# Linear attention and an MLP mixer on one core: channel mixing's weight conversion bound to the key sums of head pairs 2, 3 and 4

## The chip, the core and the metric

The kernel runs on one core of a Trainium2 chip. TensorE (PE) multiplies matrices, VectorE (DVE), ScalarE (ACT) and GpSimd (POOL) do the elementwise work, and the queue of SyncE (SP) issues most DMAs. The metric is the time of one execution on the device in microseconds (us); lower is better.

## The reference

The first half is linear attention over 8 batches and 8 heads, 576 positions and 64 features a head. `phi` maps queries and keys to 256 positive features: a product with `w_phi` (64 x 128), less its largest absolute value along the features, then the exponentials of it and of its negative.

```python
q_p, k_p = (phi(q), phi(k))
kv = np.einsum('bhsf,bhsd->bhfd', k_p, v)
z = np.sum(k_p, axis=2)
num = np.einsum('bhsf,bhfd->bhsd', q_p, kv)
den = np.einsum('bhsf,bhf->bhs', q_p, z)[..., None] + 1e-06
```

The second half takes `num / den` as x (8 x 576 x 512) through two small networks. Token mixing: u = x + (relu(x^T w_tok1) w_tok2)^T with 256 hidden units. Channel mixing: out = u + relu(u w_ch1) w_ch2 with 1536 hidden units. The four weights of the mixers come as float64.

## The kernel before, in words

Work goes by head pairs: pair i holds two heads, and four pairs make a batch, so there are 32. For a pair, `less_max` (line 184) projects keys or queries and subtracts the largest absolute value, `keys` (line 246) takes exponentials, and `add_kv` (line 276) adds the products of key features and values to the PSUM tile pkv. When a pair is through, `nc.scalar.copy` on line 298 copies the sums to the tile kv, of which there is one for each part, so the sums of the next pair are copied only when the numerators of this one have read it. `turn` (line 336) transposes the queries and takes exponentials, `numerators` (line 363) multiplies them with kv, and the denominators' reciprocals are multiplied in on line 402. For the first 4 pairs (PLAIN) this is done in plain float32; later operands are split into a high and a low part for float32r. For the first 8 pairs (EARLY) each denominator goes out to memory and back by five or six small DMAs around the reciprocal (lines 391 to 400).

`token_mix` (line 416) handles a batch in two halves, each when its two pairs are attended; `channel_mix` (line 462) handles 256 positions at a time, in six blocks of up-projection (line 478, 48 matmuls each) and of down-projection (line 493), and needs batch 0 to be mixed for its first two turns. A block reads the weights converted so far: its `until` on line 504 asks for two more chunks of `wc2`.

`convert` (line 107) turns a float64 piece of up to 128 x 512 into a high and a low float32 part. It loads it to one of four staging tiles (tags late0 to late3) by SP's queue, and then runs one absolute value on ACT (line 124), four operations of bit arithmetic on DVE (lines 125 to 128), a cast on ACT (line 65) and a subtraction on POOL (line 68). The tile that it works on is called bitsc in the profile for channel mixing's weights, the staging tile rawc. `load_weights` (line 137) calls it 7 times for token mixing's weights and then 24 times for channel mixing's, in three groups of eight (line 153): four pieces of `wc1`, four of `wc2`.

The order is set in two steps. `weave` (line 547) runs five generators side by side, keys, queries, token mixing, weight loading and channel mixing, and goes on with the one whose own clock, advanced by the cost it yields over its share, is furthest behind; a generator that yields None waits. That gives the order in which instructions are traced. From it a list scheduler with a simulated timeline places each instruction on its engine's queue: an earlier traced one goes first, and a later one may fill a slot in which its operands are ready and its engine is free in the simulation. On the chip each engine's queue runs in exactly that order.

The weight loader yields 8.0 a piece (`pace`, line 134) until pair 3 is attended, then 1.0.

Of the kernel before, what the change touches and what calls it, by code (L numbers as in the profile page):

```python
# [8 lines left out]
F32 = mybir.dt.float32  # L9
# [3 lines left out]
AF = mybir.ActivationFunctionType  # L13
# [4 lines left out]
P = 128  # L18
# [7 lines left out]
PLAIN = 4  # L26
EARLY = 8
BORROWED = 18
STAGES = 4
LAST = 15  # L30
LAG = 0.02
# [11 lines left out]
def mixer_kernel(ctx, tc, qk, vm, vt, w_phi, w1, w2, wc1, wc2d, out):  # L43
    nc = tc.nc
# [17 lines left out]
    def split(hi, lo, raw, eng_hi, eng_lo):  # L62

        if eng_hi is nc.scalar:
            nc.scalar.copy(hi, raw)
        else:
            eng_hi.tensor_copy(hi, raw)
        eng_lo.tensor_tensor(lo, raw, hi.bitcast(F32), op=ALU.subtract)
# [28 lines left out]
    for j in range(2):  # L97
        t = odd.tile([P, 5, 2, D + 1], F32, tag=f"v{j}", name=f"v{j}", bufs=1)
# [4 lines left out]
        vtiles.append(t)  # L103

    nstage = [0]

    def convert(hi, lo, srcs, name, tag=None):

        w, n = hi.shape
        if tag is None:  # L110
            tag = f"late{nstage[0] % STAGES}"
            nstage[0] += 1
        raw = wk.tile([P, 4, 256], U32, tag=tag, name=f"raw{name}", bufs=3 if tag == "xt1" else 1)
        raw = raw.rearrange("p a b -> p (a b)")[:w, :2 * n]
        at = 0
        for src in srcs:
            m = src.shape[1]
            nc.sync.dma_start(raw[:, 2 * at:2 * (at + m)].bitcast(I64), src)
            at += m
        raw = raw.rearrange("p (n two) -> p n two", two=2)  # L120
        top, low = raw[:, :, 1], raw[:, :, 0]
        m = wk.tile([P, 512], U32, tag="bits", name=f"bits{name}", bufs=3)[:w, :n]

        nc.scalar.activation(m.bitcast(F32), top.bitcast(F32), AF.Abs)
        nc.vector.tensor_scalar(m.bitcast(F32), m.bitcast(F32), LEAST, MOST, op0=ALU.max, op1=ALU.min)
        nc.vector.tensor_scalar(m, m, 3, 0x3FFFFFF8, op0=ALU.logical_shift_left, op1=ALU.bitwise_and)
        nc.vector.scalar_tensor_tensor(m, top, 0xC0000000, m, op0=ALU.bitwise_and, op1=ALU.bitwise_or)
        nc.vector.scalar_tensor_tensor(m, low, 29, m, op0=ALU.logical_shift_right, op1=ALU.bitwise_or)
        split(hi, lo, m.bitcast(F32), nc.scalar, nc.gpsimd)

    def flat(t):
        return t.rearrange("p a b -> p (a b)")

    def pace():
        return 1.0 if NP - 1 in attended else 8.0

    def load_weights():
        for u in (0, 3):
            s = UNITS[u][2]
            convert(flat(w1_h[:, u:u + 2]), flat(w1_l[:, u:u + 2]),  # L140
                    [w1[s + o:s + o + P] for o in (0, P)], f"1_{u}")
            yield 1.0
        convert(w1_h[:D, 2], w1_l[:D, 2], [w1[512:]], "1_2")
        for w in (w1_h, w1_l):
            nc.scalar.copy(w[D:, 2], w[:D, 2].bitcast(F32))
        yield 0.4
        for u in range(NT):
            rows = w2[u * P:(u + 1) * P]
            convert(w2_h[:, u, :256], w2_l[:, u, :256], [rows[:, :256]], f"2_{u}")
            yield 0.5  # L150
            convert(w2_h[:, u, 256:], w2_l[:, u, 256:], [rows[:, 512:], rows[:, 256:512]], f"3_{u}")
            yield 0.7
        for e in range(0, E, 512):
            for c in range(NC_):
                convert(wc1_h[:, c, e:e + 512], wc1_l[:, c, e:e + 512],
                        [wc1[c * P:(c + 1) * P, e:e + 512]], f"c1_{c}_{e}")
                yield pace()
            for k in range(e // P, e // P + 4):
                src = wc2d[k * P:(k + 1) * P]
                late = k - (NE - STAGES)  # L160
                if late < 0:
                    t, tag = cst.tile([P, 2, C], F32R, name=f"wc2_{k}"), None
                else:
                    t = wk.tile([P, 2, C], F32R, tag=f"late{late}", name=f"wc2_{k}", bufs=1)
                    tag = f"late{late + 1}" if late + 1 < STAGES else "xt1"
                wc2.append(t)
                convert(t[:, 0], t[:, 1], [src], f"c2_{k}", tag)
                loaded.add(k)
                yield pace()

# [13 lines left out]
    def less_max(ts, units, name, base=None):  # L184
# [4 lines left out]
        if base == D:  # L189
            ps = ps_a.tile([P, 2, 2, F], F32, tag=f"a{nplain['k'] % 2}", name=f"pp{name}")  # L190
            nplain["k"] += 1
        elif base == 0 and (nplain["q"] % 2 == 0 or nplain["q"] >= BORROWED):
            ps = ps_h.tile([P, 2, 2, F], F32, tag="h", name=f"pp{name}")
# [52 lines left out]
    def keys():  # L246
        groups = [[(0, 0), (0, 1)], [(0, 2), (0, 3)], [(1, 0), (1, 1)], [(1, 2), (1, 3)], [None]]
        todo = None
        for i in range(B * NP):
            yield from until(lambda: i < 2 or i - 2 in asked)  # L250
            if i < PLAIN:
                load_plain(i)
            else:
                load(i)
            v_sb, queue = vtiles[i % 2], nc.sync if i else nc.scalar
            queue.dma_start(v_sb[:, 0:4].rearrange("p u j d -> p (u j) d")[:, :, :D], vm[i])
            for j in range(2):
                queue.dma_start(v_sb[j * D:(j + 1) * D, 4, j, :D], vt[i, j])
            plain = D if i < PLAIN else None
            ts = pairs[i] if i < PLAIN else stack(raws[i], D, f"k{i}")  # L260
            for g, us in enumerate(groups):
                pm = less_max(ts, us, f"k{i}_{g}", plain)
                kp = wk.tile([P, 2, 2, F], F32, tag="kp", name=f"kp{i}_{g}")
                for sg in range(2):
                    nc.scalar.activation(kp[:, :len(us), sg], pm[:, :len(us)], AF.Exp, scale=1.0 - 2.0 * sg)  # L265
                yield 0.22
                if todo:
                    add_kv(*todo)
                    yield 0.82
                todo = (i, g, us, kp, v_sb)  # L270
        add_kv(*todo)
        yield 0.82
# [3 lines left out]
    def add_kv(i, g, us, kp, v_sb):  # L276
        if g == 0:
            pkvs[0] = ps_k.tile([P, 2, 2, D + 1], F32, tag="kv", name=f"pkv{i}")
        pkv = pkvs[0]
        for n, u in enumerate(us):  # L280
            for sg in range(2):
                if u is None:
                    o = pkv[:, sg].rearrange("p j d -> p (j d)")
                    v = v_sb[:, 4].rearrange("p j d -> p (j d)")
                else:
                    o, v = pkv[:, sg, u[0]], v_sb[:, u[1], u[0]]
                nc.tensor.matmul(o, kp[:, n, sg], v, start=g == 0 and n == 0 and sg == 0, stop=u is None,  # L287
                                 skip_group_check=True)
        if g < 4:
            return  # L290

        both = []
        for k in range(1 if i < PLAIN else 2):
            kv = wk.tile([P, 2, 4, D], F32 if i < PLAIN else F32R, tag=f"kv{k}", name=f"kv{k}_{i}", bufs=1)
            for at, src in ((slice(0, 4, 3), pkv[:, :, :, :D]),
                            (slice(1, 3), pkv[:, :, :, D:].to_broadcast([P, 2, 2, D]))):
                if k == 0:
                    nc.scalar.copy(kv[:, :, at], src)
                else:
                    nc.vector.tensor_tensor(kv[:, :, at], src, both[0][:, :, at].bitcast(F32), op=ALU.subtract)  # L300
            both.append(kv)
        kvs[i] = both
# [103 lines left out]
    def until(cond):  # L406
        while not cond():
            yield None
# [138 lines left out]
    def weave(streams):  # L547
# [3 lines left out]
        while streams:  # L551
# [13 lines left out]

    weave([(keys(), 5.2, True), (queries(), 5.2, True), (token_stream(), 8.0, False),
           (load_weights(), 10.0, False), (channel_stream(), 19.5, False)])


# [40 lines left out]
```

## Time and profile before

| what | value |
|---|---|
| median of 3 runs | 1162.64 us (1160.67 to 1170.23) |
| the profiled execution's own time | 1164.33 us |
| its span, first to last instruction | 1162.2 us |
| TensorE busy | 1121.3 us, 96% |
| VectorE, ScalarE, GpSimd busy | 685.7, 659.4, 570.1 us |
| matmuls | 9032 |

The profile is of one execution. PE is the matmuls, PEld the weight loads that overlap them. Names such as pkv<-v,kp are tiles, written and read, with buffer numbers left out; L298 is a line of the kernel. A float32 matmul of the plain pairs is recorded as two matmuls. Matmuls are pipelined and their ends are modelled, so a shown duration can reach beyond the start of the next; the distance between starts is the pace.

### The profile page before, as it was taken

To read this page: it belongs to the slowest core of one execution; us is meant where nothing else is said; L and a number is where in the kernel's file an instruction comes from. 1 tells how busy PE (TensorE), PEld (TensorE's weight loads), DVE (VectorE), ACT (ScalarE), POOL (GpSimd) and SP (SyncE) were. 2 spreads that over 40 slices of the span, in tenths; PEclk is the share of its full clock that TensorE was granted. 3 is DMA by queue.
4 is the path that set the end of the run, shared out by engine and by line. 5 is a ranking of instruction groups with operands and counts; after the bars stand their busy time and mean duration, and the time that the engine had idled before them with its cause. 6 is when DMAs were issued, how large, how long until landed. Compare 5 with 4: busy or idle time off the path is not lost.

```text
span 1162.2 us, 24135 instructions
## 1 busy us (share of the span) xinstructions
PE 1121.3 (96%) x9032; PEld 1090.5 (94%) x9032; DVE 685.7 (59%) x1446; ACT 659.4 (57%) x1845; POOL 570.1 (49%) x734
## 2 busy tenths in 40 slices
PE   8987799999999999999999999999999999999998
PEld 7766699998999899999999999999999989999998
DVE  7989763536656665667566465573666666553111
ACT  5678785666656665666657465563655666441110
POOL 3347773555545564566646354563554655430000
PEclk9988999999999999999999999999999999999999
DMA  8564130111111011111111011110111110000000
GB/s 224 162 187 135 42 88 24 47 43 54 32 28 52 21 41 41 32 49 32 32 49 33 19 32 50 32 50 13 38 48 33 50 31 11 20 1 19 19 19 19
DMA packets 72531, 56.77 MB, mean 49 GB/s; under 512 B 49920, under 2 KB 63648, under 8 KB 72416
## 3 DMA queue, kind: packets, MB, share of 16 engines
q1 hardware_dynamic: 71056, 54.89, 16.7%
q8 instruction: 71, 1.16, 0.4%
q10 hardware_dynamic: 1360, 0.36, 0.2%
q14 instruction: 44, 0.36, 0.1%
HBM read 45.72 MB, written 9.51 MB: 48 GB/s over the span
## 4 chain that ended last, share of the span: by engine, by line
PE 85%; ACT 5%; DVE 4%; DMA 3%; issue 1%; POOL 1%; SPq 0%; POOLq 0%; DVEq 0%; ACTq 0%
PE acc L74 25%; PE h L74 25%; PE pkv L287 9%; PE pn L74 7%; PE ph L74 4%; PE pa L74 3%; PE pt L343 3%; PE ppk L205 2%; PE ppq L205 2%; DMA inv<-few 1%; PE px L423 1%; PE pn L377 1%; PE ppk L209 1%; ACT qh L356 1%; ACT qf L350 1%
## 5 line engine op out<-in xcount | busy, mean ns | idle before, releaser
L74 PE MATMUL acc<-gh,wc 128*128 128x256 f32 x1728 | 336.5, 282 | 0.2 <-ACT gh L489 0.2
L74 PEld LDWEIGHTS acc<-gh,wc 128*128 128x128 f32 x1728 | 274.0, 189 | 0.5 <-ACT gh L489 0.4
L74 PE MATMUL h<-ul,wc_h 128*128 128x256 f32 x864 | 243.4, 282 | 1.9 <-POOL ul L470 1.8
L74 PE MATMUL h<-uh,wc_h 128*128 128x256 f32 x864 | 244.8, 284 | 0.5 <-DVE gl L490 0.5
L74 PE MATMUL h<-uh,wc_l 128*128 128x256 f32 x864 | 243.7, 282 | 0.0
L74 PE MATMUL acc<-gl,wc 128*128 128x256 f32 x864 | 242.3, 282 | 0.0
L287 PE MATMUL pkv<-v,kp 128*128 128x65 f32 (+1 forms) x1152 | 165.7, 280 | 0.4 <-ACT kp L265 0.3
L74 PEld LDWEIGHTS h<-ul,wc_h 128*128 128x128 f32 x864 | 163.1, 189 | 2.7 <-POOL ul L470 2.7
L74 PEld LDWEIGHTS h<-uh,wc_h 128*128 128x128 f32 x864 | 162.6, 188 | 1.2 <-DVE gl L490 1.1
L74 PEld LDWEIGHTS h<-uh,wc_l 128*128 128x128 f32 x864 | 163.4, 189 | 0.0
L74 PEld LDWEIGHTS acc<-gl,wc 128*128 128x128 f32 x864 | 162.8, 188 | 0.0
L287 PEld LDWEIGHTS pkv<-v,kp 128*128 128x128 f32 x1152 | 156.9, 203 | 4.0 <-issue 1.8
L265 ACT ACTIVATE kp<-pmk 128x256 f32<-128x256 f32 (+1 forms) x320 | 109.3, 392 | 89.0 <-POOL pmk L221 83.7
L357 POOL TENSOR_TENSOR ql<-qf,qh 128x320 fp32r<-128x320 f32 (+1 forms) x112 | 92.8, 828 | 135.9 <-ACT qh L356 133.2
L490 DVE SCALAR_TENSOR_TENSOR gl<-h,gh 128x512 fp32r<-128x512 f32 x108 | 74.0, 686 | 140.3 <-ACT gh L489 139.6
L350 ACT ACTIVATE qf<-pt 128x320 f32<-128x320 f32 (+1 forms) x256 | 105.2, 414 | 84.6 <-PE pt L343 83.9
L489 ACT ACTIVATE gh<-h 128x512 fp32r<-128x512 f32 x108 | 64.6, 598 | 102.5 <-PE h L74 101.8
L74 PE MATMUL pn<-qh,kv 128*128 128x320 f32 (+1 forms) x448 | 114.9, 297 | 1.7 <-DVE pq L214 0.8
L402 POOL TENSOR_TENSOR xt<-xt,den 128x320 f32<-128x320 f32 x64 | 53.8, 840 | 116.7 <-DVE den L401 36.6
L357 DVE TENSOR_TENSOR ql<-qf,qh 128x320 fp32r<-128x320 f32 (+1 forms) x112 | 71.1, 635 | 65.0 <-ACT qh L356 64.6
L221 POOL TENSOR_TENSOR pmk<-pk,mxk 128x256 f32<-128x256 f32 (+1 forms) x140 | 86.8, 620 | 30.0 <-DVE mxk L219 23.2
L180 POOL TENSOR_TENSOR stq<-raw,stq 64x512 fp32r<-64x512 f32 (+1 forms) x56 | 79.8, 1424 | 40.5 <-ACT stq L179 36.4
(109 smaller groups left out, 2420.8 us busy)
## 6 DMA issues: line engine op xcount, KB each, us to landing
raw<-in_qk SPq DMA_DIRECT2D x27, 576.0 KB, 4.0
rawc<-in_wc SPq DMA_DIRECT2D x24, 512.0 KB, 4.8
v<-in_vm SPq DMA_DIRECT2D x31, 256.0 KB, 3.9
out_x<-xt SPq DMA_DIRECT2D x12, 256.0 KB, 2.2
out_x<-xt SPq DMA_DIRECT2D x16, 192.0 KB, 2.0
raw<-in_w SPq DMA_DIRECT2D x8, 256.0 KB, 3.5
out_x<-xt SPq DMA_DIRECT2D x16, 128.0 KB, 3.0
pair<-in_qk SPq DMA_DIRECT2D x8, 160.0 KB, 3.8
```

The costliest lines, as they stand in the source:

```text
L74: nc.tensor.matmul(o, a, m, start=first and i == 0, stop=last and i == 2, skip_group_check=group_ok)
L180: nc.gpsimd.tensor_tensor(t[lo:lo + D], src, t[base:base + D].bitcast(F32), op=ALU.subtract)
L205: nc.tensor.matmul(ps[:, i].rearrange("p two f -> p (two f)"), t[:, c:c + P], wp2.rearrange("p two f -> p (two f)"), start=True, stop=True)
L221: eng.tensor_tensor(pm[:, :n], pr, mx[:, :n].unsqueeze(2).to_broadcast([P, n, F]), op=ALU.subtract)
L265: nc.scalar.activation(kp[:, :len(us), sg], pm[:, :len(us)], AF.Exp, scale=1.0 - 2.0 * sg)
L287: nc.tensor.matmul(o, kp[:, n, sg], v, start=g == 0 and n == 0 and sg == 0, stop=u is None, skip_group_check=True)
L343: nc.tensor.transpose(ptr[:, n], r, ident)
L350: nc.scalar.activation(full, src, AF.Exp, scale=1.0 - 2.0 * sg)
L357: (nc.gpsimd if sg else nc.vector).tensor_tensor(lo, full, hi.bitcast(F32), op=ALU.subtract)
L402: nc.gpsimd.tensor_tensor(x, x, den, op=ALU.mult)
L489: nc.scalar.activation(gh, ph, AF.Relu)
L490: nc.vector.scalar_tensor_tensor(gl, ph, 0.0, gh.bitcast(F32), op0=ALU.max, op1=ALU.subtract)
```

## The change

The copy of a pair's key sums is kept under the pair's number in `summed`. The loader does not trace a group of eight conversions of channel mixing's weights before pair 2's (then 3's, 4's) sums have been traced, and each conversion's first instruction, the absolute value on ACT, gets an edge that places it behind that pair's copy in ACT's queue. The edge orders one engine's own instructions and carries no semaphore. Loads and token mixing's weights are as before.

```diff
--- before.py
+++ after.py
@@ -26,6 +26,7 @@
 PLAIN = 4
 EARLY = 8
 BORROWED = 18
+FROM = 2
 STAGES = 4
 LAST = 15
 LAG = 0.02
@@ -103,8 +104,9 @@
         vtiles.append(t)
 
     nstage = [0]
-
-    def convert(hi, lo, srcs, name, tag=None):
+    summed = {}
+
+    def convert(hi, lo, srcs, name, tag=None, behind=None):
 
         w, n = hi.shape
         if tag is None:
@@ -121,7 +123,8 @@
         top, low = raw[:, :, 1], raw[:, :, 0]
         m = wk.tile([P, 512], U32, tag="bits", name=f"bits{name}", bufs=3)[:w, :n]
 
-        nc.scalar.activation(m.bitcast(F32), top.bitcast(F32), AF.Abs)
+        with tc.issue_after(summed[behind].ins) if behind is not None else nullcontext():
+            nc.scalar.activation(m.bitcast(F32), top.bitcast(F32), AF.Abs)
         nc.vector.tensor_scalar(m.bitcast(F32), m.bitcast(F32), LEAST, MOST, op0=ALU.max, op1=ALU.min)
         nc.vector.tensor_scalar(m, m, 3, 0x3FFFFFF8, op0=ALU.logical_shift_left, op1=ALU.bitwise_and)
         nc.vector.scalar_tensor_tensor(m, top, 0xC0000000, m, op0=ALU.bitwise_and, op1=ALU.bitwise_or)
@@ -151,9 +154,11 @@
             convert(w2_h[:, u, 256:], w2_l[:, u, 256:], [rows[:, 512:], rows[:, 256:512]], f"3_{u}")
             yield 0.7
         for e in range(0, E, 512):
+            pair = FROM + e // 512
+            yield from until(lambda: pair in summed)
             for c in range(NC_):
                 convert(wc1_h[:, c, e:e + 512], wc1_l[:, c, e:e + 512],
-                        [wc1[c * P:(c + 1) * P, e:e + 512]], f"c1_{c}_{e}")
+                        [wc1[c * P:(c + 1) * P, e:e + 512]], f"c1_{c}_{e}", None, pair)
                 yield pace()
             for k in range(e // P, e // P + 4):
                 src = wc2d[k * P:(k + 1) * P]
@@ -164,7 +169,7 @@
                     t = wk.tile([P, 2, C], F32R, tag=f"late{late}", name=f"wc2_{k}", bufs=1)
                     tag = f"late{late + 1}" if late + 1 < STAGES else "xt1"
                 wc2.append(t)
-                convert(t[:, 0], t[:, 1], [src], f"c2_{k}", tag)
+                convert(t[:, 0], t[:, 1], [src], f"c2_{k}", tag, pair)
                 loaded.add(k)
                 yield pace()
 
@@ -295,7 +300,7 @@
             for at, src in ((slice(0, 4, 3), pkv[:, :, :, :D]),
                             (slice(1, 3), pkv[:, :, :, D:].to_broadcast([P, 2, 2, D]))):
                 if k == 0:
-                    nc.scalar.copy(kv[:, :, at], src)
+                    summed[i] = nc.scalar.copy(kv[:, :, at], src)
                 else:
                     nc.vector.tensor_tensor(kv[:, :, at], src, both[0][:, :, at].bitcast(F32), op=ALU.subtract)
             both.append(kv)
```

## Rows read from the trace of the kernel before

**Rows 1.** The page: its head line, the busy line of the engines, and PE's row of the 40 slices of 29.06 us each (a digit is the busy share in tenths).

```profile
span 1162.2 us, 24135 instructions
PE 1121.3 (96%) x9032; PEld 1090.5 (94%) x9032; DVE 685.7 (59%) x1446; ACT 659.4 (57%) x1845; POOL 570.1 (49%) x734
...
PE   8987799999999999999999999999999999999998
```

**Rows 2.** The windows of the first 200 us, all instructions. Columns: stretch, its length, then busy us and (number) of PE, PEld (weight load), DVE, ACT, POOL, then the granted clock, the DMA share and GB/s.

```profile
27.00:57.00 30.00, 29.70 (x104) 23.47 (x103) 29.18 (x58) 20.03 (x47) 11.43 (x8) 1.00 0.60 177
57.00:75.00 18.00, 14.58 (x95) 11.65 (x93) 15.29 (x34) 16.07 (x40) 9.57 (x7) 1.00 0.57 172
75.00:100.00 25.00, 19.24 (x91) 15.50 (x91) 23.02 (x42) 16.61 (x40) 11.87 (x10) 0.80 0.68 177
100.00:125.00 25.00, 21.02 (x126) 17.82 (x126) 24.02 (x46) 20.59 (x52) 18.35 (x16) 0.90 0.37 109
125.00:145.00 20.00, 15.90 (x109) 13.81 (x109) 11.98 (x30) 16.04 (x46) 16.70 (x20) 0.96 0.08 18
145.00:165.00 20.00, 19.94 (x167) 19.73 (x167) 13.88 (x35) 15.98 (x45) 13.71 (x18) 1.00 0.30 87
165.00:200.00 35.00, 34.94 (x301) 34.74 (x301) 13.26 (x31) 22.02 (x65) 18.60 (x28) 1.00 0.13 36
```

**Rows 3.** The windows of the same stretches, only instructions that read or write the conversion's tile bitsc. Columns: stretch, its length, busy us and (number) of DVE, ACT, POOL, then clock, DMA share, GB/s of the stretch.

```profile
27.00:57.00 30.00, 22.73 (x32) 9.46 (x15) 9.42 (x6) 1.00 0.60 177
57.00:75.00 18.00, 9.34 (x13) 5.00 (x8) 5.68 (x4) 1.00 0.57 172
75.00:100.00 25.00, 19.51 (x26) 8.27 (x13) 8.99 (x7) 0.80 0.68 177
100.00:125.00 25.00, 17.95 (x21) 5.59 (x9) 6.76 (x5) 0.90 0.37 109
125.00:145.00 20.00, 0.00 (x0) 0.62 (x1) 2.57 (x2) 0.96 0.08 18
145.00:165.00 20.00, 2.21 (x4) 1.34 (x2) 1.28 (x1) 1.00 0.30 87
```

**Rows 4.** The chain of waits from 20 to 160 us, pieces in order of time: start, us, what ran.

```profile
37.74 3.60 PE pkv L287 x16
...
54.25 2.50 PE pn L377 x4
...
63.17 1.73 PE pkv L287 x16
```

**Rows 5.** Who waited for whom between 60 and 125 us: us in total, times, the longest.

```profile
PE ppq L209 <- DVE pmq L221: 5.4, 2, 3.7
...
PE ppt L209 <- DVE pmq L221: 3.4, 1, 3.4
```

**Rows 6.** The timeline of PE in the first 180 us: start, us, engine and line, operation, tiles, shapes, count, and in brackets the idle time before it and what ended it.

```profile
68.28 0.61 PE L287 MATMUL pkv<-v,kp 128*128 128x130 f32 x4
...
74.76 0.48 PE L209 MATMUL ppt<-wp,pair 64*128 64x128 f32 x2 [3.42 <-DVE pmq L221]
...
115.97 1.08 PE L377 MATMUL pn<-qf,kv 128*128 128x256 f32 x4
```

**Rows 7.** The timeline of DVE in the wait at 71 us, same columns; the instruction after these two is pmq.

```profile
71.62 1.08 DVE L127 SCALAR_TENSOR_TENSOR bitsc<-rawc,bitsc 128x512 uint32<-128x512 uint32 x1
72.62 1.75 DVE L126 TENSOR_SCALAR bitsc<-bitsc 128x512 uint32<-128x512 uint32 x1
```

**Rows 8.** The windows of 5 us behind that wait, all instructions, columns as in the second group.

```profile
75.00:80.00 5.00, 5.00 (x22) 4.38 (x22) 5.00 (x12) 2.60 (x7) 2.03 (x2) 0.54 0.79 193
80.00:85.00 5.00, 5.00 (x27) 3.98 (x26) 4.97 (x8) 2.71 (x6) 2.26 (x2) 0.78 0.99 225
```

**Rows 9.** The timeline of PE where channel mixing begins in earnest (the first of the 20 up-projection matmuls that run between 149.7 and 155 us).

```profile
149.74 0.28 PE L74 MATMUL h<-uh,wc_h 128*128 128x256 f32 x1
```

**Rows 10.** The timeline of POOL: one low-part subtraction of the key split beside the wait at 71 us, and the last product of batch 0 with its reciprocals.

```profile
72.23 1.86 POOL L180 TENSOR_TENSOR stk<-raw,stk 64x640 fp32r<-64x640 f32 x1
...
132.93 0.73 POOL L402 TENSOR_TENSOR xt<-xt,den 128x256 f32<-128x256 f32 x1 [0.86 <-DMA den<-inv]
```

**Rows 11.** The conversion's first instruction, one of its four on DVE and its last, over the whole span, by the tile bitsc: duration ns min/median/max, first and last start in us, shapes.

```profile
L124 ACT ACTIVATE bitsc<-rawc x24: 657/672/709, 27.1 to 154.4; 128x512 f32<-128x512 f32 x24
L126 DVE TENSOR_SCALAR bitsc<-bitsc x24: 408/424/1751, 28.9 to 156.3; 128x512 uint32<-128x512 uint32 x24
L68 POOL TENSOR_TENSOR wc_l<-bitsc,wc_h x12: 1269/1506/1799, 33.6 to 114.2; 128x512 fp32r<-128x512 f32 x12
```

**Rows 12.** The timeline of ACT: the copies of the key sums of pairs 2 and 3, and of pair 4 (two instructions each).

```profile
72.97 0.65 ACT L298 COPY kv<-pkv 128x256 f32<-128x256 f32 x2
...
100.62 0.64 ACT L298 COPY kv<-pkv 128x256 f32<-128x256 f32 x2
...
127.49 0.64 ACT L298 CAST kv<-pkv 128x256 fp32r<-128x256 f32 x2
```

**Rows 13.** The loads of channel mixing's weights, from the view by the tile rawc.

```profile
DMA to landing us min/median/max: 3.7/4.8/5.6
```

**Rows 14.** The window of channel mixing's first blocks, PE's instructions on the tile h alone (48 matmuls per block of up-projection). Columns: stretch, length, busy us and (number) of PE, clock, DMA share, GB/s.

```profile
120.00:214.00 94.00, 26.03 (x184) 0.98 0.18 50
```

## The prediction

> **What bounds the kernel now.** I read the busy line and the slices first [rows 1]: TensorE is busy for 96% of the span and its digit is 9 from the eighth slice (203 us) on. So a change to weight work that is over by 165 us can pay or cost only ahead of that, and I cut the start into stretches by what happens there [rows 2], with the conversions' own share of them [rows 3]. The reader is to see four things.
>
> From 27 to 57 us PE and DVE are both full: PE 29.70 of 30 us, DVE 29.18, of which 22.73 is conversion. The chain of waits says which of them sets the pace: it runs along PE, matmul to matmul [rows 4]. PE is slow there: 16 of the key-sum matmuls take 3.60 us at 37.74 and 1.73 us at 63.17. The clock column prints 1.00 for this stretch, but that spacing is the lower of the two levels (1.2 against 2.4 GHz); the rise comes at about 57 us, behind a run of numerators and transposes.
>
> From 57 to 145 us PE is no longer full: it idles 3.42, 5.76, 3.98 and 4.10 us in the four stretches, 17.3 us in all [rows 2]. The largest waits are for DVE's less-max, 5.4 and 3.4 us [rows 5]. One is seen whole at 70.9 to 74.8 us [rows 6]: PE waits for pmq, and pmq stands in DVE's queue behind two conversion instructions of 1.08 and 1.75 us [rows 7]. The clock then falls: 0.54 granted in the next 5 us, 0.78 in the 5 after [rows 8].
>
> From 125 to 145 us the DVE has no conversion work and idles 8.0 us, and in 145 to 165 us 6.1 us; POOL is at 16.70 of 20 there, against 11.43 of 30 in 27 to 57 us [rows 2, 3]. That is the room into which the change moves work.
>
> The first full block of channel mixing starts at 149.74 us, and pair 3's last numerators at 115.97 us [rows 6, 9]: between them lie the denominators (the last product by the reciprocals is at 132.93) [rows 10] and the second half of token mixing, 34 us of latency rather than of work.
>
> **What is cut, and where it goes.** No instruction is added: the edge orders instructions within ACT's own queue, where no semaphore is needed. A conversion is one DMA, one ACT absolute value, four DVE operations, one ACT cast, one POOL subtraction, 24 times [rows 11]. On DVE it took 22.73 us for 8 conversions (32 instructions) in 27 to 57 us, 2.8 us each; 19.51 for 6.5, 3.0 each, in 75 to 100; 17.95 for 5.25, 3.4 each, in 100 to 125 [rows 3]. I use 3.0.
>
> The gates: the copies of pairs 2, 3 and 4 ran at 72.97, 100.62 and 127.49 us on ACT [rows 12]. The first conversion ran at 27.1 [rows 11]; of 24, 8 were through by 57 us, 11 by 75, 18 by 100, 23 by 125. After, group 1 (eight) starts behind pair 2's copy, group 2 behind pair 3's, group 3 behind pair 4's. Loads carry no edge; four may still land early into the four staging tiles, but the fifth waits on SP until a first conversion frees one, and behind it on SP's queue stand pair loads and the denominators' small DMAs. A load took 4.8 us to land [rows 13], and the weights' absence lightens 27 to 65 us; I cost the queue at nothing, bounds 2 us either way (about half a landing).
>
> *27 to 57 us.* DVE loses 22.7 us of work and ACT 9.5, but PE had only 0.3 us of idle time there: I take 0. Bounds: 0 and a gain of 10.5, if the clock rises in the middle of the stretch (21 us of work done at double speed). A loss has no place, since nothing is put there.
>
> *57 to 85 us.* Pair 2's sum needs PE work that is through at 68.9 us [rows 6], and its copy stood 4 us behind on an ACT that did 5.0 us of conversion in 57 to 75 [rows 3, 12]. With DVE free until that copy, no conversion lies ahead of pmq at 71 to 74 us. The gap's 3.4 us go, and so do the two cold stretches behind it: (1-0.54)/0.5 x 5 us at half speed lose 2.3 us, (1-0.78)/0.5 x 5 us lose 1.1 [rows 8]. Sum 6.8 us, bounds 0 (the stall comes again behind the first conversions of group 1) and 6.8; I take it whole, since the backlog that made it cannot exist yet. What is late next is the numerators, waiting for ACT's exponentials.
>
> *85 to 125 us.* Before, 10 to 12 conversions ran here. After, groups 1 and 2 are allowed from some 68 and 95 us; 16 x 3.0 = 48 us at the share that conversions had of DVE (19.51 of 25, 78%) take 62 us, until 130. Same density, so 0. Bounds: a gain of 9.7 (all PE idle time of 75 to 125 us) and a loss of 5.4 (one more wait of the largest kind [rows 5]).
>
> *125 to 165 us.* Here conversion is new: 8 more, 24 us of DVE, against 14.1 us idle up to 165 and 21.7 more up to 200 [rows 2]. They aren't needed in that time: channel mixing's fifth block of up-projection, the first to read group 3, starts only at about 214 us (184 of the first 192 matmuls stand before it) [rows 14]. What it costs is blocking: the second half of token mixing has ten DVE steps in a row (five splits, one for the middle layer, four sums), and each finds an instruction of 0.65 us in its way, half of it on average: 10 x 0.33 = 3.3, I take 3.0. Bounds: 0, and 16 (24 less DVE's 8.0 of idle time to 145 us, all of it on PE). POOL's 8 x 1.4 = 11 us [rows 11] go into 9.6 us of idle time; at nothing, as they end no wait before 214 us, with 2 us of loss if the reciprocal products queue behind them.
>
> Which of DVE's operations stretch is seen in one place: L126 took 0.42 us in the median and 1.75 us at 72.62, ending with the POOL subtraction that ran from 72.23 for 1.86 us [rows 7, 10, 11]. The Trainium skill, "SBUF — State Buffer", section "Who interferes with whom", says that a VectorE instruction with two SBUF inputs, or in a two-port mode, shares a port pair with GpSimd and that the later of the two blocks fully. That rule speaks against moving conversions to where POOL is 84% busy; the trace agrees on the one case, and with the 3.4 us that a conversion took in 100 to 125 us, where POOL was at 73%, the added load would be 27 us instead of 24: some 3 us more loss in the sum.
>
> **Sum**, on the profiled execution of 1164.3 us (span 1162.2 and 2.1 around it): 1164.3 - 6.8 + 3.0 = 1160.5. The median of the three runs is 1162.6, 1.7 lower, which would make 1158.9; I say 1160.
>
> **Rivals.**
> A, the forecast above: 37%.
> B, *the clock rises early.* Every run of numerators and transposes before 57 us is a chance for it, and the one at 54.25 us took it [rows 4]. Without conversions a faster PE finds DVE with 6.5 us of other work in 30, so it could keep the pace; before, it could not have. 10.5 us, and with pair 2's sum that much earlier group 1 is over before the queries of pair 3, so half of the 5.76 us idle in 75 to 100: 1164.3 - 6.8 - 10.5 - 2.9 + 3.0 = 1147. Against it: PE's order in that stretch is dense already and its work is the same. 30%.
> C, *nothing moves that matters*: PE's pace covers the first group, the stall at 71 us returns behind the first conversions of group 1, and group 3 fits in the idle time: 1164. 13%.
> D, *the far end pays.* DVE in 125 to 165 us needs 12.0 + 11.7 us for its other work and 24 for group 3, 47.7 of 40: 7.7 us too much, and if each of the ten token-mixing steps waits a whole instruction (0.65) 6.5 more; the stall at 71 us returns too: 1164.3 + 14.2 = 1178. It decides from about the sixth conversion behind 125 us on (16.3 us idle over 3.0). For it: DVE has been full for as long as there were conversions. Against: PE is full from 145 us with other work. 20%.
>
> **Numbers.** Two runs of this kernel can be told apart from about 1% on, 11.6 us. A alone has 1150 to 1169. The range reaches past B's 1147 by the 5 or 6 us of idle time it leaves in 75 to 125, to 1141, and just past D's 1178, to 1179. Faster by over 1%: 8 in 10 of B, 15% of A, little of C: 0.30. Slower: 8 in 10 of D, 8% of A, 10% of C: 0.21. Within: 0.49.
>
> **What would show it.** Right: no conversion before pair 2's copy, that copy at 66 to 70 us, no PE gap above 3 us at 70 to 75; pair 3's last numerators at 109 to 113 and the first full block of channel mixing at 144 to 149 us; the last conversion between 155 and 190. Key-sum matmuls at half rate until about 57 us as before: A; full rate from 40 us on: B. DVE at 19 of 20 us in 125 to 165 with PE waiting on L68, L428 or L458: D. The forecast is wrong if PE's idle time before 165 us changes by more than 8 us, or if the time moves and the first 200 us did not.

## The result, and the profile after

The changed kernel takes 1176.18 us in the median of 20 runs (1171.16 to 1183.92) against 1166.76 of the kernel before (20 runs beside it, 1160.67 to 1175.48): a ratio of 1.0077 [1.0053, 1.0101]. It is slower by 0.8%, where the record had it 0.2% faster. Its profiled execution took 1176.14 us, 11.8 us more than that of before.

The page of the changed kernel: its head line, the busy line, and PE's row of the 40 slices.

```profile
span 1174.1 us, 24131 instructions
PE 1117.5 (95%) x9032; PEld 1088.2 (93%) x9032; DVE 695.4 (59%) x1446; ACT 659.6 (56%) x1845; POOL 575.1 (49%) x734
...
PE   8987779998999999999999999999999999999998
```

Against [rows 1] DVE is 9.7 us busier with the same 1446 instructions. The difference in time lies in the first 200 us, as these windows of all instructions show (columns as in [rows 2]); the kernel before first, then the changed one.

```profile
0.00:200.00 200.00, 178.37 (x1075) 156.56 (x1076) 150.43 (x324) 141.25 (x365) 108.80 (x125) 0.96 0.45 124
```

```profile
0.00:200.00 200.00, 165.20 (x973) 145.37 (x974) 156.49 (x315) 134.66 (x343) 108.83 (x113) 0.88 0.44 123
200.00:400.00 200.00, 192.41 (x1620) 189.80 (x1619) 111.08 (x248) 123.72 (x357) 110.13 (x150) 1.00 0.15 40
```

At 200 us the changed kernel has done 102 matmuls fewer. From 200 to 400 us one takes 192.41 / 1620 = 0.119 us, so 102 are 12.1 us, near the 11.9 us by which the span grew. DVE in those 200 us was busy longer (156.49 against 150.43) with fewer instructions (315 against 324).

The same by the stretches of the record's sum; before, then after.

```profile
27.00:57.00 30.00, 29.70 (x104) 23.47 (x103) 29.18 (x58) 20.03 (x47) 11.43 (x8) 1.00 0.60 177
57.00:85.00 28.00, 24.58 (x140) 20.01 (x139) 25.26 (x52) 21.38 (x52) 13.85 (x10) 0.88 0.68 185
85.00:125.00 40.00, 30.26 (x169) 24.96 (x169) 37.07 (x68) 31.88 (x79) 25.94 (x22) 0.89 0.43 126
125.00:165.00 40.00, 35.84 (x275) 33.54 (x274) 25.86 (x64) 32.02 (x90) 30.42 (x38) 0.98 0.19 52
165.00:200.00 35.00, 34.94 (x301) 34.74 (x301) 13.26 (x31) 22.02 (x65) 18.60 (x28) 1.00 0.13 36
```

```profile
27.00:57.00 30.00, 28.83 (x195) 23.57 (x193) 15.76 (x48) 20.46 (x57) 3.72 (x4) 1.00 0.35 102
57.00:85.00 28.00, 24.15 (x115) 19.79 (x115) 20.08 (x41) 21.89 (x55) 13.35 (x11) 0.76 0.46 128
85.00:125.00 40.00, 27.63 (x165) 23.42 (x164) 39.80 (x72) 30.00 (x76) 32.89 (x29) 0.91 0.52 150
125.00:165.00 40.00, 29.01 (x157) 26.77 (x158) 39.80 (x64) 27.62 (x69) 29.95 (x28) 0.74 0.42 123
165.00:200.00 35.00, 32.56 (x252) 32.00 (x252) 21.27 (x41) 20.84 (x55) 20.36 (x22) 0.90 0.12 31
```

Read DVE's column down. Before, it is full first and has room later; after, it idles 14.2 us in 27 to 57 and is full, 39.80 of 40, twice over from 85 to 165. PE's count in 125 to 165 falls from 275 to 157, at a clock of 0.74 on the mean.

What a stretch loses on PE can be estimated as its idle time plus (1 - clock) times its length, with the busy time and the clock of the rows above (time in which PE idles at the low clock counts twice). Before: 57 to 85 us 3.4 + 3.4, 85 to 125 9.7 + 4.4, 125 to 165 4.2 + 0.8, 165 to 200 0.1. After: 3.9 + 6.7, 12.4 + 3.6, 11.0 + 10.4, 2.4 + 3.5. The changes are +3.8, +1.9, +16.4 and +5.8, together +27.9. From 27 to 57 us the changed kernel is ahead, because its clock rose at about 29 us: before, 30 us at half rate lost 15 and the idle time 0.3; after, some 2.4; a gain of some 13. The balance is some 15 us where the span grew by 11.9; an estimate with double counting comes no nearer. In 125 to 165 us a second trace of each kernel repeats it: before (1161.5 us) PE idled 4.3 us at a clock of 0.99, after (1173.05 us) 8.0 us at 0.66, with DVE at 39.80 of 40 again, 21.6 us lost on PE (21.4 in the first).

The conversions' share, by the tile bitsc in the changed kernel (columns as in [rows 3]):

```profile
27.00:57.00 30.00, 0.00 (x0) 0.00 (x0) 0.00 (x0) 1.00 0.35 102
57.00:75.00 18.00, 7.20 (x14) 4.71 (x8) 3.62 (x3) 0.72 0.37 114
75.00:100.00 25.00, 20.14 (x21) 6.49 (x11) 6.32 (x5) 0.93 0.54 148
100.00:125.00 25.00, 17.53 (x23) 7.00 (x11) 9.12 (x6) 0.86 0.53 153
125.00:145.00 20.00, 15.46 (x16) 4.39 (x7) 5.89 (x4) 0.59 0.43 123
145.00:165.00 20.00, 12.45 (x13) 5.47 (x9) 5.33 (x5) 0.90 0.41 123
```

From 75 to 165 us they take 65.6 us of DVE, against 39.7 in [rows 3]: 25.9 more. Over the kernel, the conversions' 96 DVE operations took 82.86 us in all, before 71.74. The last of the four shows the stretching (columns as in [rows 11], where L128 is L131 now):

```profile
L131 DVE SCALAR_TENSOR_TENSOR bitsc<-rawc,bitsc x24: 674/827/2016, 63.6 to 176.3; 128x512 uint32<-128x512 uint32 x24
```

How other work stands behind them, in the timeline of DVE in the changed kernel:

```profile
115.93 1.76 DVE L131 SCALAR_TENSOR_TENSOR bitsc<-rawc,bitsc 128x512 uint32<-128x512 uint32 x1
117.61 0.68 DVE L130 SCALAR_TENSOR_TENSOR bitsc<-rawc,bitsc 128x512 uint32<-128x512 uint32 x1
118.22 1.15 DVE L362 TENSOR_TENSOR ql<-qf,qh 128x320 fp32r<-128x320 f32 x1
119.29 0.68 DVE L131 SCALAR_TENSOR_TENSOR bitsc<-rawc,bitsc 128x512 uint32<-128x512 uint32 x1
119.89 0.41 DVE L219 TENSOR_TENSOR pq<-ppq,partq 128x256 f32<-128x256 f32 x1
120.23 0.41 DVE L219 TENSOR_TENSOR pk<-ppk,partk 128x256 f32<-128x256 f32 x1
```

pq and pk take 0.41 us each; the 4.0 us from 115.93 to 119.89 ahead of them went to four others, three of them of conversions. PE's longest wait in total is for pk; who waited for whom in 75 to 185 us (us in total, times, the longest), in place of [rows 5]:

```profile
PE ppk L210 <- DVE pk L219: 9.6, 6, 2.4
PE pn L75 <- DVE pq L219: 3.5, 1, 3.5
PE pa L438 <- DVE xs L433: 2.6, 2, 1.3
PE ph L75 <- DVE xt L463: 2.6, 2, 1.3
PE ph L75 <- DVE al L454: 2.0, 2, 1.5
```

The copies of the key sums on ACT, pairs 1 to 4, in place of [rows 12]:

```profile
42.80 0.64 ACT L303 COPY kv<-pkv 128x256 f32<-128x256 f32 x2
58.72 0.64 ACT L303 COPY kv<-pkv 128x256 f32<-128x256 f32 x2
78.28 0.65 ACT L303 COPY kv<-pkv 128x256 f32<-128x256 f32 x2
109.93 0.63 ACT L303 CAST kv<-pkv 128x256 fp32r<-128x256 f32 x2
```

Pairs 2 to 4 lead by 14.3, 22.3 and 17.6 us. Yet the last sum of batch 0's token mixing comes at 154.62 us against 151.18: the lead of 22.3 us at pair 3 has become a lag of 3.4. These 25.7 us are lost in the time in which 25.9 us more of conversion lie; that the two are so close may be chance. The first conversion began at 59.4 us and the ninth at 94.45, the seventeenth at 128.3: both of them 16 to 18 us behind the copy that frees them. So in this execution only the first group's gate, pair 2, held anything back directly: its conversion ran 0.7 us behind the copy.

### The profile page after: what moved, and what is told of

The parts are those of the page before. It is cut to its first block, busy times and chain, and to the rows that moved or that the text cites. A ratio compares the mean times of both kernels' runs of the same rounds, so it can differ in the third digit from the quotient of the medians.

```text
span 1174.1 us, 24131 instructions
## 1 busy us (share of the span) xinstructions
PE 1117.5 (95%) x9032; PEld 1088.2 (93%) x9032; DVE 695.4 (59%) x1446; ACT 659.6 (56%) x1845; POOL 575.1 (49%) x734
## 4 chain that ended last, share of the span: by engine, by line
PE 82%; DVE 7%; ACT 5%; DMA 3%; issue 2%; POOL 1%; SPq 0%; POOLq 0%; DVEq 0%; ACTq 0%
PE h L75 24%; PE acc L75 24%; PE pkv L292 9%; PE pn L75 7%; PE ph L75 3%; PE pt L348 3%; PE pa L75 2%; PE ppk L210 2%; PE ppq L210 2%; DVE bitsc L130 2%; PE pn L382 1%; DVE bitsc L128 1%; DVE bitsc L131 1%; PE px L428 1%; PE ppk L214 1%
## 5 line engine op out<-in xcount | busy, mean ns | idle before, releaser
L185 POOL TENSOR_TENSOR stk<-raw,stk 64x512 fp32r<-64x512 f32 (+1 forms) x56 | 81.2, 1449 | 39.7 <-ACT stk L184 28.5
```

The source lines that it names most:

```text
L185: nc.gpsimd.tensor_tensor(t[lo:lo + D], src, t[base:base + D].bitcast(F32), op=ALU.subtract)
```

## The experiments

Theory 1, which came out of this: DVE is the limit from the first conversion to about 170 us; the edge moves 72 us of its work from a start at 27 to one at 59 us, and what attention gains ahead is spent behind. Rivals: the clock's rise; the new order in which instructions are traced; contention with POOL; the place in DVE's queue. The expectations number them as they came up. Ratios are to the kernel before, run beside each, with the 95% interval. The kernel before took 1167.1, 1169.4, 1173.4 and 1168.1 us in the median of the four comparisons, so ratios of different comparisons can differ by half a per cent for that alone.

**The same two kernels again** (no edit: before three times, after once, one execution each for its trace).

> The kernel before once more, for its trace. If the moment at which the clock rises is set by chance, this trace has its key-sum matmuls of 28 to 57 us at either rate, and the time to 57 us is not tied to it, since DVE is full either way. If the change made the clock rise early, this trace is at the low rate until about 57 us as the first was.

> The changed kernel once more, for its trace. The second trace of the kernel before had the clock rise at 29 us with pair 2's copy at the same time as in the first, so the moment is chance. Here, should it rise late, pair 2's copy and with it the first conversion come at about 70 us instead of 59, and the time is near 1180; should it rise early again, 1171 to 1177.

> A third trace of the kernel before. If low clock is what parts its runs: a run above 1168 us shows a stretch of low clock between 55 and 80 us that the traces of 1164 and 1161 us lack, and pair 2's copy near 83 us instead of 73; a run below 1166 us shows pair 2's copy near 73.

> A fourth trace of the kernel before, with the same two readings as the third: above 1168 us, low clock between 55 and 80 us; below 1166 us, none.

Before took 1161.5, 1170.68 and 1166.29 us, after 1173.05. Read from the spacing of the key-sum matmuls, the clock rose at about 30, 60 and 30 us in before, and at 30 in after. In the first of them 16 of these matmuls took 2.00 us at 34.52 us (3.60 at 37.74 in [rows 4]); then PE waited:

```profile
34.52 2.00 PE L287 MATMUL pkv<-v,kp 128*128 128x65 f32 x16
...
41.41 2.08 PE L377 MATMUL pn<-qf,kv 128*128 128x256 f32 x4 [4.25 <-ACT qf L350]
```

The copies of pairs 1 to 4 in the same trace:

```profile
52.54 0.64 ACT L298 COPY kv<-pkv 128x256 f32<-128x256 f32 x2
72.52 0.65 ACT L298 COPY kv<-pkv 128x256 f32<-128x256 f32 x2
99.22 0.64 ACT L298 COPY kv<-pkv 128x256 f32<-128x256 f32 x2
126.24 0.64 ACT L298 CAST kv<-pkv 128x256 fp32r<-128x256 f32 x2
```

With the clock up some 28 us earlier pair 2's copy came at 72.52 instead of 72.97: the early PE idled 5.4 us of 30 to 60, and its clock fell back (0.72 on the mean there). So when the clock rises differs from execution to execution of this program, and PE alone doesn't set the pace in 27 to 57 us. The wait of 4.25 us is for ACT; DVE was busy all 6.00 us from 36 to 42, ACT 4.41, so DVE's part is argued from its being full. The third trace of before missed its expectation: it was slow without a low clock at 55 to 80 us and with pair 2's copy at 75.13; it was 2 us behind from the start and lost 3.4 more to the clock at 140 to 160. What cost it that stays open.

**The edges away, the trace order kept** (twice).

```diff
-                convert(t[:, 0], t[:, 1], [src], f"c2_{k}", tag, pair)
+                convert(t[:, 0], t[:, 1], [src], f"c2_{k}", tag)
```

The call for wc1 loses its pair in the same way.

> The groups are traced behind the sums as in the change, but the absolute values carry no edge. The scheduler fills free slots with whatever is ready, so ACT's queue has the conversions where the kernel before has them, the first at about 27 us: 0.997 to 1.003 under every theory. A loss like the change's would mean that the order of tracing makes it.

> The kernel without the edge once more. If its 0.65% on the first chip is its own (all of its ten runs had a mean clock of 0.984 to 0.990, while more than half of the runs of the kernel before lay below 0.978): 0.991 to 0.998 again. If it was that chip: 0.998 to 1.002.

1165.51 us, 0.9935 [0.9907, 0.9964], and 1165.25, 0.9964 [0.9933, 0.9994]. The first conversion began at 26.9 and 29.8 us. The first of the two, by the tile bitsc:

```profile
27.00:60.00 33.00, 25.33 (x35) 10.68 (x17) 11.57 (x8) 0.84 0.54 161
...
75.00:165.00 90.00, 43.78 (x50) 15.73 (x25) 19.89 (x15) 0.91 0.38 102
```

Conversions are back in the early time, 43.8 us instead of 65.6 remain for 75 to 165, and the loss is gone. So the edge costs, and not the order in which things are traced. The conversions' DVE operations are stretched here too (77.9 us in all, 75.8 in the second trace, before 71.7), so stretching alone doesn't make the loss. This version beats both kernels, before by 0.4 to 0.65%, in the first comparison more than was expected under any theory. Both comparisons ran on one chip, so whether the gain is the chip's own stays untested.

Part of that lies with before, as the runs' mean granted clock shows. The 100 runs of before beside the experiments (one more, of 3609 us, is left out) fall into two groups, 58 at 0.980 or less with a median of 1172.8 us and 42 above it with 1165.1. Of the 22 runs without edges 21 are above 0.980, with 1165.4 in the median of all; of the 21 of the changed kernel three are, at 1173 to 1180 us, and the other 18 have a median of 1176.1. So the version without edges is as fast as the upper group of before and seldom falls into the lower, and the changed kernel is only 3.3 us slower than before's own lower group. The four traces of before are all of its upper group. Whether a run of its lower group loses time as the changed kernel does, so that the edge in part only makes such executions more frequent, isn't tested, and what makes a run fall into one group or the other stays open.

**Less DVE work in each conversion**, in the kernel before and in the changed one.

```diff
-        nc.vector.scalar_tensor_tensor(m, top, 0xC0000000, m, op0=ALU.bitwise_and, op1=ALU.bitwise_or)
-        nc.vector.scalar_tensor_tensor(m, low, 29, m, op0=ALU.logical_shift_right, op1=ALU.bitwise_or)
```

> The kernel before, with two of the four DVE operations of every conversion left out (the sign and the low bits of the weights are missing): 1.35 us of some 3.0 each. Theory 1: DVE no longer bounds the stretch from 57 to 145 us, so most of the 26 us that PE loses there (idle and low clock) goes: 0.985 to 0.993 times before. Rival 3 (weights come late, whatever the DVE does): 1.00.

> The changed kernel with the same two DVE operations of every conversion left out. Theory 1: with conversions at half the DVE time the late start costs little: within 0.3% of the light kernel before. Rival 2 (POOL beside conversion): between, about 0.4% above the light kernel before. Rival 3 (the late gate itself holds up channel mixing): still 0.8% above the light kernel before.

1155.52 us, 0.9906 [0.9872, 0.994], and 1160.57, 0.9943 [0.9912, 0.9975]. Their quotient is 1.0037, half of the loss and just what rival 2 gave; theory 1 gave at most 0.3%. With the two intervals taken together it is 0.999 to 1.008. Taken directly against each other, 10 runs and 8, the means differ by 4.8 us with an interval of 1.6 to 8.1, 0.1 to 0.7%: some loss remains, and that it is smaller than the whole one (0.5 to 1.0%) is likely but not shown. Their traces, both of runs near their medians, agree. The windows of 60 to 180 us of before, after, light before, light after:

```profile
60.00:180.00 120.00, 102.62 (x689) 90.44 (x689) 92.86 (x191) 94.97 (x248) 79.37 (x80) 0.93 0.39 109
```

```profile
60.00:180.00 120.00, 92.26 (x512) 81.54 (x510) 111.86 (x192) 84.06 (x209) 84.46 (x75) 0.80 0.42 120
```

```profile
60.00:180.00 120.00, 103.45 (x720) 93.85 (x721) 59.77 (x150) 89.16 (x237) 71.68 (x79) 0.93 0.29 76
```

```profile
60.00:180.00 120.00, 98.72 (x628) 89.02 (x629) 81.21 (x162) 95.39 (x244) 83.91 (x85) 0.86 0.44 130
```

In these 120 us PE does 177 matmuls of 689 fewer with the edge and the whole conversion, 92 of 720 fewer with the light one. With the gain ahead counted in, from 0 to 200 us, it is 102 and 61 fewer (1093 of 1154). Less DVE work, less loss, in one trace of each.

**The conversion without POOL**, in both kernels.

```diff
-        split(hi, lo, m.bitcast(F32), nc.scalar, nc.gpsimd)
+        nc.scalar.copy(hi, m.bitcast(F32))
+        nc.scalar.copy(lo, m.bitcast(F32))
```

> The kernel before with the conversions' low part written by a copy on ACT instead of the subtraction on POOL (so the low parts hold the wrong numbers): 31 POOL operations of 1.4 us are gone, 31 ACT copies of 0.6 us are added. Base for the next run. Theory 1, DVE being the limit: 0.990 to 1.000, as DVE is held up less. Rival 2: 0.985 to 0.992.

> The changed kernel with the same replacement on ACT. Theory 1: DVE still has its 72 us of conversion and the same late start: 0.6 to 0.9% above the same kernel without the gates. Rival 2 (POOL's share of the conversion, and its holding up DVE, make the loss): within 0.3% of it.

1163.42 us, 0.9957 [0.9934, 0.9981], and 1171.22, 1.0015 [0.9982, 1.0048]: a quotient of 1.0058, 1.002 to 1.010 with the intervals together. The loss stays, so POOL's own part of a conversion isn't its cause. The conversions' DVE time was 56.1 and 69.2 us in the traces: 13.1 of stretching remain, with POOL busy at other work. But these traces don't show the loss. They are of the slowest run of the first kernel (1165.98 us) and the fastest of the second (1162.05), and the second is 13 matmuls behind at 200 us (1052 of 1065), with DVE at 38.24 of 40 in 125 to 165 and the clock at 0.82. So the edge, the late conversions and their stretching don't cost the whole 0.6% in every execution.

**Other gates.** First, each group one pair earlier:

```diff
-FROM = 2
+FROM = 1
```

> The groups are bound to pairs 1, 2 and 3 instead of 2, 3 and 4. Theory 1 (DVE is what the first 170 us wait for, and DVE time left idle before the first conversion is not regained): the first conversion starts at about 43 us instead of 59 (before: 27), DVE idles some 8 us between 30 and 60 us (16.1 after, 1.8 before), and the loss is about half of the change's: 1.003 to 1.006 times before. Rival 2 (what costs is conversion beside a busy POOL, each of its DVE operations held up): the DVE time of the 24 conversions, 71.7 us before and 82.9 after, comes out near 77, and the time follows that and not the idle time. Rival 3 (the gates of the second and third group hold weights back from channel mixing): no change against after, 1.008, or worse where the second and third gate bind.

1172.28 us, 1.006 [1.0029, 1.0091]. The time is theory 1's, but not for its reason: the first conversion began at 52.0 us in the trace (1178.6 us, slower than most of its runs) and not at 43, DVE idled 15.0 of 30 to 60 and not 8, almost as much as the 16.1 of the changed kernel, and the conversions took 83.2 us of DVE and not 77. The interval also holds rival 3's 1.008, so this run decides little.

Then the first group free and the others held by pairs 3 and 4 (`if not e: pair = None`), and only the third held, by pair 4 (`if e < 1024: pair = None`), which was traced twice:

> The first group of eight is free, as before; only the second and third are bound to pairs 3 and 4. Theory 1 (DVE time left idle early is what is lost): the first eight run in 27 to 57 us as before, then DVE idles some 15 to 20 us until pair 3's copy at about 75 to 80 us, as much as the change leaves idle ahead of its first conversion, so 1.005 to 1.009 times before. Rival 2 (a conversion costs more where POOL is busy): sixteen instead of 24 conversions are moved late, two thirds of the change's loss, 1.005. Rival 4 (the clear run for the attention of pairs 2 and 3 is worth more than the wait, only that of pair 1 is not): 0.995 to 1.00.

> Only the third group of eight is bound, to pair 4's sums; the first sixteen are as before. Theory 1: DVE is idle from about 90 us, where the first sixteen end, to pair 4's copy at 110 to 115, some 10 us, partly used by a faster attention: 1.000 to 1.004. Rival 2: eight conversions run beside a busy POOL in 115 to 165 us: 1.003, and DVE time of the conversions near 76 us. The record's term for late conversions alone, 3 us or 0.3% of blocking, would be seen here by itself.

> A second trace of the kernel with only the third group bound. If the stretch of low clock at 60 to 80 us in its first trace was chance, a run below 1175 us shows pair 2's copy near 73 us; DVE's idle time between the sixteenth conversion and pair 4's copy, 12 us, and the loss of 8 us stay.

The first free: 1186.21 us (6 runs), 1.0139 [1.0098, 1.018], more than theory 1 had given it. In its trace, which is of its fastest run (1175.27 us), DVE idles 11.2 us of 60 to 80 and 5.2 of 80 to 100, and is full behind (19.8 and 19.9 of 20 us): the same hole, later. The price of the other five runs, 1180 us and more, is higher than its size explains and has no trace. The third alone: 1178.43, 1.0067 [1.0037, 1.0096], more than theory 1's 1.000 to 1.004, and 1179.62 in the second traced run. Its conversions did not stretch (71.6 us of DVE in the first trace). What it has is a PE full at the low clock, in both traces:

```profile
60.00:80.00 20.00, 20.00 (x72) 15.32 (x71) 11.14 (x25) 10.57 (x28) 5.68 (x5) 0.50 0.47 151
```

```profile
60.00:80.00 20.00, 20.00 (x73) 15.28 (x72) 11.25 (x24) 10.58 (x28) 5.69 (x6) 0.50 0.48 151
```

Ten of these 20 us are lost, and pair 2's copy comes at 83.43 and 83.21 us. The first trace is of the slowest run (1186.18 us), and it need not be so in every run: seven of the twelve, this one among them, have a mean clock of 0.971 or less and take 1178 to 1186 us, five have 0.975 or more and take 1169 to 1175. Why the clock stays down there, and how a gate at pair 4 brings it about, is open.

**Gates at other places**: the third group alone, behind the last copy of uh in channel mixing's first turn; and groups 2 and 3 behind the middle layers of token mixing.

```diff
+            pair = {0: None, 512: None, 1024: ("uh", 0)}[e]
```

```diff
+            pair = {0: None, 512: ("mid", 0, 0), 1024: ("mid", 0, 1)}[e]
```

The lines that enter these instructions into `summed` are left out here.

> The first two groups are free as before; the third is bound to ACT's last copy for channel mixing's first turn (uh), so none of its DVE work stands ahead of batch 0's last token-mixing sum: 64 conversion operations do in DVE's queue, against 92 before and 78 after. Theory 5 (the first turn of channel mixing starts when DVE has come through what its queue puts ahead of that sum): 28 operations of 0.75 us less, so the sum ends at 138 to 146 us instead of 151, and the eight late conversions fall into 145 to 200 us, where DVE had 30 us of idle time: 0.992 to 0.999 times before. Rival 2' (a conversion that is late costs, wherever it stands, as in the run with only the third group bound): 1.003 to 1.008.

> The second group is bound to the middle layer of token mixing's first half, the third to that of the second half: 72 conversion operations stand ahead of the last sum. Theory 5 with theory 1: DVE is idle between the first group and the second, from about 60 to 100 us, and the sixteen come late and full in 100 to 180: 1.000 to 1.008. Rival 4 (the attention of pairs 2 and 3 alone without conversions is worth most): 0.990 to 0.998.

1174.06 us, 1.0028 [0.9997, 1.006], and 1179.51, 1.0057 [1.0026, 1.0088]. The first puts 64 of the 96 conversion operations ahead of batch 0's last token-mixing sum in DVE's queue (before 92, after 78), and that sum comes at 157.2 us, later than in either, where theory 5 had 138 to 146: a place in the queue alone doesn't explain the time. Its trace (1181.46 us, one of its slower runs) has the low clock at 60 to 80 us as well. The second lies in theory 1's range and shows the mechanism at its plainest:

```profile
60.00:80.00 20.00, 19.02 (x102) 15.46 (x102) 7.46 (x22) 11.24 (x32) 5.94 (x6) 0.76 0.45 135
80.00:100.00 20.00, 19.75 (x117) 16.22 (x117) 7.54 (x22) 14.47 (x41) 5.32 (x6) 0.90 0.15 33
...
120.00:140.00 20.00, 14.51 (x66) 11.51 (x64) 19.94 (x35) 13.38 (x36) 14.28 (x15) 0.67 0.47 137
140.00:180.00 40.00, 33.30 (x225) 32.04 (x226) 39.76 (x65) 26.96 (x67) 31.26 (x28) 0.84 0.33 97
```

While DVE idles, PE is nearly full; then DVE is full for 60 us and PE is not, and the clock is lower.

## Why the prediction was wrong

The likeliest case did not come; what came is rival D's loss, paid in part by B's early clock.

*27 to 57 us, forecast 0: about -13.* The record read from the chain that PE sets the pace and hides the conversions. Half of that is so: with the clock up early and the conversions in place pair 2's copy came no earlier (72.52), so PE was not the only limit. Free of conversions, a PE at full rate runs ahead, 42.80 instead of 53.55 us at pair 1. B priced this at 10.5 and had its mechanism right. Both traces of after had the early clock, but the kernel with each group one pair earlier, as free of conversions there, did not (about 46 us, pair 1's copy at 51.32): the gain isn't the change's alone, and that it came in the profiled execution is luck.

*57 to 85 us, forecast -6.8: +3.8.* The stall at 71 us did go, and no gap above 3 us stands at 70 to 75; pair 2's copy came at 58.72, before the 66 to 70 that were named. But PE idled behind that copy, and the clock was down after it:

```profile
59.42 1.77 PE L382 MATMUL pn<-qf,kv 128*128 128x320 f32 x4 [1.77 <-ACT kv L303]
```

From 60 to 70 us PE was full at 0.51, 4.9 us lost. The record took one stall's removal for the removal of such stalls.

*85 to 125 us, forecast 0: +1.9.* Right, inside its bounds. Two groups were to be through at 130 us; the seventeenth conversion began at 128.3.

*125 to 165 us, forecast +3.0: +16.4, and +5.8 behind.* This step failed, and it decides the sign. The record had the work right, 24 us more conversion on DVE (15.46 + 12.45 - 2.21 = 25.7), and even D's sum, 47.7 us wanted of 40. It then priced ten steps that each wait half an instruction, which supposes an engine with room. This one was full, and its other work was put off: DVE did 39.80 - 27.9 = 11.9 us of it in these 40, before 25.86 - 2.2 = 23.7. The next pair's pk, for which PE waited 9.6 us in 75 to 185 us, is not among the ten steps at all. On top PE ran at a granted clock of 0.74 there (10.4 us lost), which the record counted behind the stall at 71 us and nowhere here. POOL and the loads, put at nothing, don't bear it: POOL was at 29.95 of 40 us (before 30.42), and ACT waited once for a load of a weight, 2.8 us (before four times, 5.7).

D had this mechanism, DVE overfull, at 20%, and its 1178 lies 2 us from the measured time, in part by luck. It priced the end at 14.2 where 22.2 were lost (16.4 and 5.8); it had no loss by the clock, and the return of the stall at 71 us, which it had, did not come. The gain of some 13 us at the start, which it hadn't, made up for that. Its argument against, that PE is full from 145 us with other work, fails because that work comes later too: channel mixing's first block starts with one matmul at 152.13 us and goes on from 154.68 (149.74, [rows 9], and 150.56 before; 144 to 149 forecast), although pair 3's last numerators ran at 99.37 (115.97 in [rows 6]; 109 to 113 forecast).

*Signs and readings.* PE's digit in [rows 1] is 9 from the sixth slice (145 us) on and not the eighth; nothing in the sum rests on it. PE's idle time from 27 to 165 us went from 17.6 to 28.4 us, more than the 8 that the record set as its limit. DVE was at 39.80 of 40 in 125 to 165 and PE waited on xs and xt (L433, L463 now): D's. The key-sum matmuls ran at full rate from 40 us on: B's. The last conversion began at 164.5 us, inside 155 to 190.

The Trainium skill, "SBUF — State Buffer", section "Who interferes with whom", has a VectorE instruction with two SBUF inputs contend with a GpSimd instruction that reads SBUF. The trace agrees in direction: with POOL's subtraction the conversions of before took DVE 71.7 us, without it 56.1. The 3 us that the record worked out for eight conversions were left out of its sum; all 24 conversions took 11.1 more in the changed kernel.

Shown: that the edge costs and not the trace order (the kernel without it at 0.9935 and 0.9964), the place (the first 200 us), and in both traces of after a full DVE beside a PE that idles and runs at a lower clock. Supported, but not beyond the noise: that the loss goes with DVE's work per conversion. Open: the low clock at 60 to 80 us of the kernels that hold back the third group alone, the size of the loss with only the first group free, what parts the two groups of runs of before, and how much of the change's loss is more runs of the lower one.

## What to carry to other kernels

Hold filler work back only into time in which its engine has room for it and for all that will be there: add up that engine's whole demand behind the new start, not the filler's own share. Where two engines are full together, the chain of waits may name only one of them, and a gain from freeing the other lasts until the work put off comes due. An engine that would be overfull is priced by the work that it puts off, and by the clock that PE's new gaps cost, not by half an instruction per step.

## What was not expected of the hardware

In four traces of the same program the clock rose from its lower to its upper level inside the group of key-sum matmuls that began at 57.18, 28.48, 59.30 and 29.89 us: up to some 30 us apart, though PE runs the same instructions in the same order. A PE busy 20.00 of 20 us stayed at a granted clock of 0.50 all that time in three traces (60 to 80 us, two kernels that hold back only the third group). And one DVE operation on 128x512 integers took from 0.67 to 2.02 us in one execution.
